# Layer two's weights through two buffers, products and last steps in another order, x loaded in pieces

## The chip, the cores and the metric

The kernel runs on one core of a Trainium2 chip. The core has a matrix engine (TensorE, PE in the rows; its weight loads are PEld), a vector engine (VectorE, DVE), a scalar engine (ScalarE, ACT), GpSimd (POOL) and SyncE (SP), which here issues nearly all DMAs. Each engine runs its own list of instructions in order, and semaphores tie the lists together. 16 DMA engines move the data between HBM and the core's on-chip memory. The metric is the device time of one execution in microseconds (us).

## What is computed

```python
x = attention(q, k, v)                # 4 batches, 8 heads, 576 rows, 64 columns; two kinds of window
x = x.transpose(0, 2, 1, 3).reshape(2304, 512)
h = x @ moe_w_in                      # 512 x 2048
x = (h - np.tanh(h)) @ moe_w_out      # 2048 x 512: layer one
h = x @ moe2_w_in                     # 512 x 2048
out = (h * (1 / (1 + np.exp(-h)))) @ moe2_w_out   # layer two
```

The weights come as 64-bit floats, which the kernel converts. Each operand of a product is held as two parts, a leading and a trailing one, and a product is three matmul passes (trailing with leading, leading with leading, leading with trailing): `passes`, L563.

## The kernel before

**Attention and layer one** come first. The 2304 tokens of layer one are cut into five blocks, four of 512 tokens and one of 256. For each block 16 slots run (f = 0 to 15), one for each 128 columns of w_in. In a slot PE makes h (12 matmuls, `hidden`), then the y products of the slot before (12 matmuls, `run_second`); ACT takes tanh (L589), DVE subtracts (L590), ACT copies the leading part of gg (L1213) and DVE subtracts the trailing part (L1215). At a block's end the four y banks in PSUM are cleared by ACT (L622) and DVE (L623) into x and stored to y1_hi and y1_lo.

**The feed stage.** Beside layer one's blocks 3 and 4 (340 to 455 us of the profile) layer two's w_in is prepared, and the results are stored to HBM as w2_in. `in_steps(i)` is called once in a slot, behind the slot's other work in the program. Each call converts one chunk of 128 columns (ACT L175 and L180, DVE L185, POOL L189, in the tile st_in). Two chunks make a pair q. On an even i the pair's three plain parts (ACT L1125 and L1126) and four sums and differences, the tile "mixed" (DVE L1128 and L1111), are made, the plain parts' trailing halves follow on DVE, the next two chunks are loaded, and plain is stored (L1137, L1138). On the odd i that follows the leading and trailing parts of mixed are made (ACT L1140, DVE L1111), and it is stored (L1142). So a pair is two slots and seven DMAs on SP's queue: four loads of 256 KB, two stores of 256 and 512 KB, one store of 1024 KB. There is one tile "mixed" and one tile "plain"; a pair can only write them when the last pair's stores have read them.

**Layer two** runs in three groups of 768 tokens, with the Winograd form of Strassen's scheme: seven products where eight would be needed. For each of eight quads (pairs of w_in chunks) `products` runs 7 products of 6 matmuls of 384 columns in the order 1, 6, 5, 7, 2, 3, 4 (`ORDER`); 1 and 2 add up in the bank a (h), 6 in b (q0), 5 and 3 in c (q1), 7 and 4 in d (y3). `sums` and `add` take values of the banks between the products (DVE L699): the sum with d has to read 7 alone, before 4 is added. In the first quad of the first group the last y products of layer one stand between the first three products and the others. Then 16 steps (f = 0 to 15, `second`) make the group's six output tiles, with 3 matmuls of 512 columns for each tile and step; `split` makes the leading and trailing parts gs of a later step (ACT L728, DVE L729), two steps ahead. In the last group steps 14 and 15 are run together, tile by tile. At the end each tile is copied (ot; ACT L756, DVE L754, or both for the last one) and stored.

**x of the next group.** While a group's 16 steps run, `load` fetches the next group's x (two halves XR[0] and XR[1], a leading and a trailing part of each, 768 KB a piece) and `mixes` returns 16 small steps (DVE L661, L665, L671; ACT L668) that make the operands "side" 5, 6 and 7, and the combined side 4 in place. The weights of each product or step are fetched to tiles wr by `fetch`, some steps ahead. In group 0 the w_out of layer two is also still being converted: each step there stores one converted chunk (room) and loads a raw one.

## Time and profile before

| | us |
|---|---|
| median of 3 runs | 873.75 |
| the runs | 871.97 to 874.69 |
| the profiled execution | 874.53 |
| its span, first to last instruction | 872.8 |
| PE busy in it | 849.9 |
| DVE, ACT, POOL busy | 521.0, 404.7, 125.3 |

The profile page gives busy times, the span in 40 slices, DMA queues, the chain of work that ended last, and groups of instructions by line. The trace behind it can be asked for one stretch, engine or line: what ran in order of time, and which wait preceded it. A row's duration on PE is modelled at its end; two rows in a sequence start closer together than the first one's duration says, so times on PE are best taken from start to start. "Idle before" in square brackets is how long the engine stood still before the row, and what ended that.

### The profile page before, as it was taken

The numbers are of one execution on the slowest core, as the hardware profiler recorded it, in microseconds if no ns is written. First come the engines' busy times: TensorE is split into PE (matmuls) and PEld (weight loads), VectorE is DVE, ScalarE is ACT, GpSimd is POOL, SyncE is SP. The second block draws the span as 40 slices with busy tenths as digits, with TensorE's granted clock in tenths as the row PEclk, the third lists the DMA queues.
The fourth block names the chain that finished last, engine by engine and source line by source line (L and its number), as shares of the span: only waits on it lengthen the run. The fifth ranks groups of instructions, "written<-read, shape, count | busy, mean of one in ns | idle before, by whom it ended". The sixth has DMA issues, their size and how long they took to land.

```text
span 872.8 us, 14406 instructions
## 1 busy us (share of the span) xinstructions
PE 849.9 (97%) x5287; PEld 730.0 (84%) x5287; DVE 521.0 (60%) x942; ACT 404.7 (46%) x939; POOL 125.3 (14%) x165
## 2 busy tenths in 40 slices
PE   8999999999999999998989999999999999999997
PEld 5777887888888888876779999887999888999885
DVE  3788996366677553655474677645666453566222
ACT  5899974344343433645443355663334231333112
POOL 8555441011000000111100011120000000000000
PEclk9999999999999999999999999999999999999999
DMA  9987263223342103675559199999796930998002
GB/s 233 273 225 182 68 152 122 67 49 56 63 129 50 36 21 97 229 255 184 224 225 379 62 371 375 335 385 366 265 407 229 359 111 2 350 359 266 1 0 73
DMA packets 148870, 166.63 MB, mean 191 GB/s; under 512 B 87840, under 2 KB 114496, under 8 KB 147776
## 3 DMA queue, kind: packets, MB, share of 16 engines
q1 hardware_dynamic: 147968, 164.86, 57.2%
q0 software_dynamic: 832, 0.85, 0.4%
q8 instruction: 42, 0.69, 0.3%
q14 instruction: 28, 0.23, 0.1%
HBM read 128.45 MB, written 37.22 MB: 190 GB/s over the span
## 4 chain that ended last, share of the span: by engine, by line
PE 76%; DMA 7%; ACT 7%; DVE 6%; issue 2%; SPq 2%; POOL 0%; DVEq 0%; ACTq 0%; POOLq 0%
PE y L563 34%; PE h L563 20%; PE q L563 15%; DMA w_in<-mixed 5%; DMA wr<-w_out 1%; ACT prob L454 1%; PE s L401 1%; PE h L495 1%; DVE g L590 1%; DVE x L623 1%; SPq L328 1%; ACT st L175 1%; DVE mixed L1111 1%; ACT mixed L1140 1%; PE o L401 1%
## 5 line engine op out<-in xcount | busy, mean ns | idle before, releaser
L563 PE MATMUL y<-gg,w 128*128 128x512 f32 (+1 forms) x960 | 220.8, 373 | 9.9 <-DVE gg L1215 9.9
L563 PE MATMUL h<-x,w 128*128 128x512 f32 (+1 forms) x960 | 218.8, 370 | 1.5 <-DVE g L590 0.9
L563 PEld LDWEIGHTS y<-gg,w 128*128 128x128 f32 x960 | 168.3, 190 | 44.6 <-DVE gg L1215 12.8
L563 PEld LDWEIGHTS h<-x,w 128*128 128x128 f32 x960 | 167.1, 189 | 33.3 <-POOL w L198 1.1
L563 PE MATMUL y<-wr,gs 128*128 128x512 f32 x576 | 139.6, 390 | 1.1 <-DMA wr<-w_out 0.6
L563 PEld LDWEIGHTS y<-wr,gs 128*128 128x128 f32 x576 | 107.9, 188 | 24.5 <-issue 1.0
L729 DVE TENSOR_TENSOR gs<-G,gs 128x768 fp32r<-128x768 f32 x48 | 45.7, 958 | 103.1 <-ACT gs L728 103.1
L728 ACT ACTIVATE gs<-G 128x768 fp32r<-128x768 f32 x48 | 40.3, 845 | 106.0 <-PE y L563 106.0
L708 ACT ACTIVATE G<-tmp 128x384 f32<-128x384 f32 x72 | 37.7, 526 | 102.1 <-DVE tmp L699 95.1
L563 PE MATMUL q<-x,wr 128*128 128x384 f32 x432 | 82.6, 334 | 0.0
L1213 ACT ACTIVATE gg<-g 128x512 fp32r<-128x512 f32 (+1 forms) x64 | 37.0, 578 | 94.9 <-DVE g L590 94.9
L563 PEld LDWEIGHTS q<-x,wr 128*128 128x128 f32 x432 | 75.6, 188 | 0.0
L563 PE MATMUL q<-wr,gs 128*128 128x512 f32 x288 | 72.9, 389 | 0.0
L589 ACT ACTIVATE g<-h 128x512 f32<-128x512 f32 (+1 forms) x64 | 34.7, 541 | 77.1 <-PE h L563 67.8
L590 DVE TENSOR_TENSOR g<-h,g 128x512 f32<-128x512 f32 (+1 forms) x64 | 39.7, 620 | 42.9 <-ACT g L589 42.4
L1215 DVE TENSOR_TENSOR gg<-g,gg 128x512 fp32r<-128x512 f32 (+1 forms) x64 | 40.1, 626 | 41.3 <-ACT gg L1213 39.9
L563 PEld LDWEIGHTS q<-wr,gs 128*128 128x128 f32 x288 | 54.1, 188 | 11.3
L563 PE MATMUL y<-x,wr 128*128 128x384 f32 x288 | 57.7, 334 | 0.9 <-DVE x L623 0.9
L563 PE MATMUL h<-x,wr 128*128 128x384 f32 x288 | 57.7, 334 | 0.0
L699 DVE TENSOR_TENSOR tmp<-tmp,q 128x384 f32<-128x384 f32 x72 | 39.7, 552 | 20.1 <-PE q L563 16.0
L563 PEld LDWEIGHTS y<-x,wr 128*128 128x128 f32 x288 | 50.6, 188 | 1.1 <-DVE x L623 1.1
L563 PEld LDWEIGHTS h<-x,wr 128*128 128x128 f32 x288 | 50.6, 188 | 0.2
(124 smaller groups left out, 975.4 us busy)
## 6 DMA issues: line engine op xcount, KB each, us to landing
wr<-w_in SPq DMA_DIRECT2D x72, 512.0 KB
wr<-w_out SPq DMA_DIRECT2D x48, 512.0 KB
st<-in_moe_w_in_dram SPq DMA_DIRECT2D x32, 256.0 KB
st<-in_moe_w_out_dram SPq DMA_DIRECT2D x16, 512.0 KB
st_in<-in_moe_w_in_dram SPq DMA_DIRECT2D x32, 256.0 KB
w_in<-mixed SPq DMA_DIRECT2D x8, 1024.0 KB
raw<-in_moe_w_out_dram SPq DMA_DIRECT2D x16, 512.0 KB
w_out<-room SPq DMA_DIRECT2D x16, 512.0 KB
```

Of the source, the lines that this page charges most:

```text
L175: engine.activation(out=high, in_=high, func=AF.Prelu, scale=2.0 ** -112, alpha=2.0 ** 32)
L328: out.append(lambda e, n=n, p0=p0, r=r, i=i, m=m: e.dma_start(out=self.vt[p0:p0 + m, :, n, :], in_=src[r, i:i + m]))
L401: nc.tensor.matmul(s[QB * j:QB * (j + 1), m, at:at + size], self.qT[64 * j:64 * j + 64, QB * n:QB * n + QB], self.kT[64 * j:64 * j + 64, k ...
L563: nc.tensor.matmul(o, stat[a], mov[b], start=first and n == 0, stop=last and n == 2, skip_group_check=more)
L589: nc.scalar.activation(out=g, in_=h, func=AF.Tanh)
L590: nc.vector.tensor_tensor(out=g, in0=h, in1=g, op=ALU.subtract)
L699: nc.vector.tensor_tensor(out=out, in0=a, in1=b, op=ALU.add)
L708: nc.scalar.activation(out=g, in_=h, func=AF.Tanh, scale=0.5)
L728: nc.scalar.activation(out=gs[:, 0], in_=g, func=AF.Copy)
L729: nc.vector.tensor_tensor(out=gs[:, 1], in0=g, in1=gs[:, 0].bitcast(F32), op=ALU.subtract)
L1213: nc.scalar.activation(out=gg[:, 0], in_=g, func=AF.Copy)
L1215: nc.vector.tensor_tensor(out=gg[:, 1], in0=g, in1=gg[:, 0].bitcast(F32), op=ALU.subtract)
```

## The change

1. mixed and plain get two tiles each, used by pairs in turn (q % 2).
2. In the first quad of the first group (`begins`) the products after layer one's last y run in the order 2, 3, 7, the sum with d, 4, instead of 7, the sum, 2, 3, 4.
3. `load` becomes `loads`, a list of four; XR[1] is loaded before XR[0], and the leading and the trailing part of one half follow each other. For group 0's own x all four are still issued together. For the next group's x one piece is issued in each of four steps, from step 5 on in group 0 (all four were issued at 7) and from step 0 on in group 1. Two mixing steps are run in each step from 8 on in group 0 (three each from 10 on before) and from 3 on in group 1 (two each from 2 on before).
4. Where two steps are run together (the last two of the last group), their parts are sorted: two tiles of step 14 run ahead of the first of step 15, and the tiles of the two steps alternate from there.
5. `dynamic_dma_scratch_size` is 2048 where it was 4096.

```diff
@@ -633,11 +633,12 @@
         def __init__(self, s):
             self.s, self.t0, self.G = s, 2 * HALF * s, []
 
-        def load(self):
-            for a, src in ((0, y1_hi), (1, y1_lo)):
-                for r, t in zip(XR, (self.t0, self.t0 + HALF)):
-                    nc.sync.dma_start(out=X[:, a, :, r].bitcast(F32),
-                                      in_=src[:, :, t:t + HALF].rearrange("c p t -> p c t"))
+        def loads(self):
+            def load(a, src, r, t):
+                return lambda: nc.sync.dma_start(out=X[:, a, :, r].bitcast(F32),
+                                                 in_=src[:, :, t:t + HALF].rearrange("c p t -> p c t"))
+
+            return [load(a, src, r, t) for r, t in zip(XR[::-1], (self.t0 + HALF, self.t0)) for a, src in ((0, y1_hi), (1, y1_lo))]
 
         def sides(self):
             a, b = (slice(0, 2), slice(2, 4))
@@ -736,11 +737,14 @@
                 self.y = [(ps_q.tile([P, 512], F32, tag=f"q{c - 3}", name=f"q{c - 3}") if c in (3, 4) else
                            ps_y.tile([P, 512], F32, tag=f"y{min(c, 3)}", name=f"y{min(c, 3)}")) for c in range(nt)]
             ws = [coming.pop(0) for _ in parts]
-            for c in range(nt):
+            order = [(c, k) for c in range(nt) for k in range(len(parts))]
+            if len(parts) > 1:
+                order.sort(key=lambda x: (x[0] + 2 * x[1], x[1]))
+            for c, k in order:
                 o = self.y[c]
-                for (f, gs), w in zip(parts, ws):
-                    passes(o, [gs[:, a, c * P:(c + 1) * P] for a in range(2)], [w[:, a] for a in range(2)],
-                           f == 0, f == NF - 1)
+                f, gs = parts[k]
+                passes(o, [gs[:, a, c * P:(c + 1) * P] for a in range(2)], [ws[k][:, a] for a in range(2)],
+                       f == 0, f == NF - 1)
                 if f == NF - 1:
                     ot = wpool.tile([P, DM], F32, tag="wout", name="ot")
                     t, p = self.t0 + c * P, 0
@@ -1119,6 +1123,7 @@
 
             q = i // 2 - 1
             own = 0 <= q < NF // 2
+            mixed, plain = mixes2[q % 2], plains[q % 2]
             if own and i % 2 == 0:
                 a, b = sides(q)
                 both = WIN[2 * q].high.bitcast(F32)
@@ -1173,8 +1178,8 @@
                 fpool = feeding.enter_context(tc.tile_pool(name="feed", bufs=1, reuse_waits="tile"))
                 ps_q = ctx.enter_context(tc.tile_pool(name="ps_q", bufs=1, space=PSUM, reuse_waits="tile"))
                 st_in = fpool.tile([P, 4, 2, DM // 2, 2], U32, name="st_in")
-                mixed = fpool.tile([P, 4, 2, 2 * P], F32R, name="mixed")
-                plain = fpool.tile([P, 3, 2, 2 * P], F32R, name="plain")
+                mixes2 = [fpool.tile([P, 4, 2, 2 * P], F32R, tag=f"mixed{k}", name="mixed") for k in range(2)]
+                plains = [fpool.tile([P, 3, 2, 2 * P], F32R, tag=f"plain{k}", name="plain") for k in range(2)]
                 for k in range(4):
                     WIN[k].load(st_in[:, k])
                 began = NF * (t - 1) + f + 1
@@ -1221,7 +1226,7 @@
                         in_steps(i - began)
                     if t == len(blocks) - 1:
                         if f == 4:
-                            groups[0].load()
+                            run(groups[0].loads())
                             mixing = groups[0].mixes()
                         if 5 < f < 14:
                             fetch()
@@ -1247,9 +1252,13 @@
                     begins = False
                     while waiting:
                         run_second()
-                u.products(quad, u.ORDER[3:4])
-                u.add(u.t[:, 1], u.t[:, 1], u.d)
-                u.products(quad, u.ORDER[4:])
+                    u.products(quad, (2, 3, 7))
+                    u.add(u.t[:, 1], u.t[:, 1], u.d)
+                    u.products(quad, (4,))
+                else:
+                    u.products(quad, u.ORDER[3:4])
+                    u.add(u.t[:, 1], u.t[:, 1], u.d)
+                    u.products(quad, u.ORDER[4:])
                 for _ in range(4 if u.s or quad < NF // 2 - 2 else 2):
                     fetch()
                 if quad == NF // 2 - 1:
@@ -1275,13 +1284,16 @@
                     out_split(k - 1)
                     out_steps(k)
                     out_load(k + 2)
-                if after and f == (0 if u.s else 7):
-                    after.load()
-                    mixing = after.mixes()
-                if f > (1 if u.s else 9):
-                    for _ in range(2 if u.s else 3):
-                        if mixing:
-                            mixing.pop(0)()
+                first = 0 if u.s else 5
+                if after and f == first:
+                    loading, mixing = after.loads(), after.mixes()
+                if after and f >= first:
+                    if loading:
+                        loading.pop(0)()
+                    if f > first + 2:
+                        for _ in range(2):
+                            if mixing:
+                                mixing.pop(0)()
             run(mixing)
 
 
@@ -1296,7 +1308,7 @@
     from concourse import mybir as _mybir
     from concourse.bass_utils import run_bass_kernel_spmd as _run
 
-    nc = _bacc.Bacc("TRN2", target_bir_lowering=False, num_devices=1, dynamic_dma_scratch_size=4096)
+    nc = _bacc.Bacc("TRN2", target_bir_lowering=False, num_devices=1, dynamic_dma_scratch_size=2048)
     arrays, args = {}, []
     for name in _INS:
         a = _np.ascontiguousarray(inputs[name])
```

Where instructions move, in the lists of the two programs:

DVE's list in the feed stage, the second pair (q = 1), before. L1128 is the first write to mixed, the L1111 with two halves (2x256) the first to plain; in square brackets are the queues that the instruction waits for (DMAHW: a DMA's).

```order
L1128 TENSOR_TENSOR mixed<-st_in 128x256 [waits DMAHW6_49,Pool_49]
L1111 TENSOR_TENSOR mixed<-st_in 128x256
L1111 TENSOR_TENSOR mixed<-mixed,st_in 128x256 [waits DVE_49]
L1111 TENSOR_TENSOR mixed<-st_in,mixed 128x256 [waits DVE_49]
L1111 TENSOR_TENSOR plain<-st_in,plain 128x2x256 [waits DMAHW5_49,DMAHW4_49,Activation_49]
L1111 TENSOR_TENSOR plain<-st_in,plain 128x256 [waits Activation_49]
L185 TENSOR_SCALAR st_in<-st_in 128x512 [waits DMAHW1_49,DMAHW0_49,Activation_49]
L590 TENSOR_TENSOR g<-h,g 128x512 [waits Activation_49]
L1215 TENSOR_TENSOR gg<-g,gg 128x512 [waits PE_49,Activation_49]
```

The same place now:

```order
L1133 TENSOR_TENSOR mixed<-st_in 128x256 [waits Pool_49]
L1115 TENSOR_TENSOR mixed<-st_in 128x256
L1115 TENSOR_TENSOR mixed<-mixed,st_in 128x256 [waits DVE_49]
L1115 TENSOR_TENSOR mixed<-st_in,mixed 128x256 [waits DVE_49]
L1115 TENSOR_TENSOR plain<-st_in,plain 128x2x256 [waits Activation_49]
L1115 TENSOR_TENSOR plain<-st_in,plain 128x256 [waits Activation_49]
L185 TENSOR_SCALAR st_in<-st_in 128x512 [waits DMAHW1_49,DMAHW0_49,Activation_49]
L590 TENSOR_TENSOR g<-h,g 128x512 [waits Activation_49]
L1220 TENSOR_TENSOR gg<-g,gg 128x512 [waits PE_49,Activation_49]
```

The order stays; the waits for the stores (DMAHW6; DMAHW5 and 4) are gone from this pair, and the third pair's L1133 waits for the store of the first.

DVE's list at the end of group 0, before: the last of the mixing steps (L661, L665, L671), the copies ot of three output tiles (L754), and the first sums of group 1 (L699). The L671 of 128x768 ahead of ot makes the trailing part of side 6, the one of 128x2x384 that of side 4.

```order
L671 TENSOR_TENSOR x_4370<-tmp,x_4370 128x768
L661 TENSOR_TENSOR tmp<-x 128x768
L665 TENSOR_TENSOR tmp<-tmp 128x768
L671 TENSOR_TENSOR x_4370<-tmp,x_4370 128x768
L754 TENSOR_SCALAR ot<-y_5503 128x512
L754 TENSOR_SCALAR ot<-q_5505 128x512
L754 TENSOR_SCALAR ot<-y_5507 128x512
L671 TENSOR_TENSOR x<-tmp,x 128x2x384
L699 TENSOR_TENSOR tmp<-tmp,q_6003 128x384
```

The same place now:

```order
L672 TENSOR_TENSOR x_4372<-tmp,x_4372 128x768
L662 TENSOR_TENSOR tmp<-x 128x768
L666 TENSOR_TENSOR tmp<-tmp 128x768
L758 TENSOR_SCALAR ot<-y_5505 128x512
L758 TENSOR_SCALAR ot<-q_5507 128x512
L758 TENSOR_SCALAR ot<-y_5509 128x512
L672 TENSOR_TENSOR x_4372<-tmp,x_4372 128x768
L672 TENSOR_TENSOR x<-tmp,x 128x2x384
L700 TENSOR_TENSOR tmp<-tmp,q_6005 128x384
```

Side 6's trailing part has moved behind the three copies.

PE's list in the last two steps of the last group, before (step 14's first tile, then step 15's first tile, then both steps' parts of each tile, six matmuls a row):

```order
L563 MATMUL y_7562<-wr,gs 128x512 [waits DMAHW5_49,Activation_49]
L563 MATMUL y_7562<-wr,gs 128x512
L563 MATMUL y_7562<-wr,gs 128x512 [waits DVE_49]
L563 MATMUL y_7562<-wr,gs 128x512 [waits DMAHW6_49,Activation_49]
L563 MATMUL y_7562<-wr,gs 128x512
L563 MATMUL y_7562<-wr,gs 128x512 [waits DVE_49]
L563 MATMUL y_7563<-wr,gs 128x512 x6
L563 MATMUL y_7564<-wr,gs 128x512 x6
L563 MATMUL q_7565<-wr,gs 128x512 x6
L563 MATMUL q_7566<-wr,gs 128x512 x6
L563 MATMUL y_7567<-wr,gs 128x512 x6
```

The same place now, from step 14's first tile on:

```order
L563 MATMUL y_7564<-wr,gs 128x512 [waits DVE_49]
L563 MATMUL y_7565<-wr,gs 128x512 x3
L563 MATMUL y_7566<-wr,gs 128x512 x3
L563 MATMUL y_7564<-wr,gs 128x512 [waits DMAHW6_49,Activation_49]
L563 MATMUL y_7564<-wr,gs 128x512
L563 MATMUL y_7564<-wr,gs 128x512 [waits DVE_49]
L563 MATMUL q_7567<-wr,gs 128x512 x3
L563 MATMUL y_7565<-wr,gs 128x512 x3
L563 MATMUL q_7568<-wr,gs 128x512 x3
L563 MATMUL y_7566<-wr,gs 128x512 x3
L563 MATMUL y_7569<-wr,gs 128x512 x3
```

Two tiles of step 14 now stand between its first tile and the waits for step 15's gs; the rest of the list (not shown) ends with step 15's parts of the last three tiles.

## Rows read from the trace of the kernel before

**Rows 1.** The page: busy us, share, instructions; PE's granted clock in 40 slices.
```profile
PE 849.9 (97%) x5287; PEld 730.0 (84%) x5287; DVE 521.0 (60%) x942; ACT 404.7 (46%) x939; POOL 125.3 (14%) x165
...
PEclk9999999999999999999999999999999999999999
```

**Rows 2.** Waits of PE (340-500 us) and DVE (340-460): us, times, longest.
```profile
PE y L563 <- DVE gg L1215: 9.1, 5, 1.9
...
DVE mixed L1128 <- DMA w_in<-mixed: 26.6, 7, 5.9
```

**Rows 3.** PE in order of time, feed stage: start, us, instruction, count, idle before.
```profile
379.69 2.88 PE L563 MATMUL y<-gg,w 128*128 128x512 f32 x12
382.41 2.88 PE L563 MATMUL h<-x,w 128*128 128x512 f32 x12
386.76 3.01 PE L563 MATMUL y<-gg,w 128*128 128x512 f32 x12 [1.46 <-DVE gg L1215]
389.61 2.88 PE L563 MATMUL h<-x,w 128*128 128x512 f32 x12
...
425.99 4.61 PE L563 MATMUL y<-gg,w 128*128 128x512 f32 x12 [1.89 <-DVE gg L1215]
430.43 2.90 PE L563 MATMUL h<-x,w 128*128 128x512 f32 x12
```

**Rows 4.** Busy by window: PE, PEld, DVE, ACT, POOL, granted clock, DMA share, GB/s.
```profile
427.00:428.00 1.00, 1.00 (x4) 0.81 (x3) 0.92 (x3) 0.79 (x2) 0.12 (x1) 0.50 0.80 232
```

**Rows 5.** The same view, two pairs of the feed stage, unstalled and stalled.
```profile
352.00:363.00 11.00, 11.00 (x50) 9.09 (x50) 7.74 (x15) 6.84 (x12) 2.28 (x3) 1.00 0.90 316
...
410.00:423.00 13.00, 11.11 (x49) 8.88 (x48) 6.95 (x14) 6.37 (x11) 2.08 (x2) 1.00 0.62 222
```

**Rows 6.** In order of time, from block 3 to block 4.
```profile
446.08 0.42 DVE L1128 TENSOR_TENSOR mixed<-st_in 128x256 f32<-128x256 f32 x1 [1.52 <-DMA w_in<-mixed]
...
450.62 2.41 PE L563 MATMUL y<-gg,w 128*128 128x256 f32 x12
...
453.90 1.69 PE L563 MATMUL h<-x,w 128*128 128x256 f32 x12 [0.86 <-DVE g L590]
...
455.42 1.60 PE L563 MATMUL y<-gg,w 128*128 128x256 f32 x12
```

**Rows 7.** In order of time, the first quad of group 0 (product 7 at 498.50).
```profile
498.50 1.31 PE L563 MATMUL y<-x,wr 128*128 128x384 f32 x6 [0.93 <-DVE x L623]
...
499.65 1.20 PE L563 MATMUL h<-x,wr 128*128 128x384 f32 x6
499.85 0.55 DVE L699 TENSOR_TENSOR tmp<-tmp,y 128x384 f32<-128x384 f32 x1 [1.40 <-PE y L563]
...
500.69 1.20 PE L563 MATMUL q<-x,wr 128*128 128x384 f32 x6
```

**Rows 8.** Group 0, step 12: a window's busy times; then in order of time.
```profile
560.00:580.00 20.00, 20.00 (x90) 16.57 (x89) 9.16 (x15) 12.38 (x21) 5.20 (x5) 1.00 1.01 386
...
592.50 1.73 SPq L1103 DMA_DIRECT2D wr<-w_out  x1
...
603.51 2.32 PE L563 MATMUL y<-wr,gs 128*128 128x512 f32 x9 [0.62 <-DMA wr<-w_out]
```

**Rows 9.** In order of time, from group 0 to group 1.
```profile
620.15 0.69 DVE L754 TENSOR_SCALAR ot<-y 128x512 f32<-128x512 f32 x1 [0.67 <-PE y L563]
620.76 0.95 DVE L671 TENSOR_TENSOR x<-tmp,x 128x768 fp32r<-128x768 f32 x1
...
621.02 2.24 PE L563 MATMUL q<-x,wr 128*128 128x384 f32 x12
```

**Rows 10.** PE in order of time, the last two steps.
```profile
858.29 1.52 PE L563 MATMUL y<-wr,gs 128*128 128x512 f32 x6
860.06 0.73 PE L563 MATMUL y<-wr,gs 128*128 128x512 f32 x2 [0.26 <-ACT gs L728]
861.05 3.24 PE L563 MATMUL y<-wr,gs 128*128 128x512 f32 x13 [0.26 <-DVE gs L729]
```

## The prediction, as it was put on record

> **What bounds the kernel now.** First the page: TensorE (PE) is busy 849.9 of 872.8 us, so at most some 23 us of idle can go, and its granted clock is full in nearly every slice [rows 1]. No edit here removes a matmul; the change can only win what PE waits for, and the slow matmuls that follow a wait. So the next view is PE's waits by stretch. From 340 to 500 us, the stage in which layer two's input weights are prepared beside layer one's blocks 3 and 4, PE waits 9.1 us for the vector engine's (DVE's) gg, in five stops, and the views of the other engines in that stage name what is behind: DVE stands 26.6 us at L1128, the first write to "mixed", until the DMA that stores the last pair's mixed has landed [rows 2]. Its queue runs in order. The gate of the next slot (L590, L1215) is queued behind L1128, and PE's y matmuls wait for the gate's gg. Then PE in order of time shows the size of a stop: 12 matmuls of 512 columns start 2.72 us after the 12 ahead of them (379.69 to 382.41), but the y at 386.76 starts 4.35 us after the h at 382.41, so 1.63 are lost [rows 3]. The last stage is read in the same way at its few stops.
>
> **Part 1, the two buffers (feed stage).** The five stops: 9.1 us of idle, plus 0.16 each, since the view counts a row of 12 as 2.88 long and the next starts after 2.72: 9.1 + 0.8 = 9.9. After a stop the first 12 take 0.13 longer (386.76 to 389.61 is 2.85 against 2.72), four times: 0.5. After the fourth stop the 12 at 425.99 take 4.44 us (to 430.43), 1.72 too many [rows 3]; the granted clock there reads 0.50, that is 1.2 of 2.4 GHz, after the 1.89 us in which PE stood idle [rows 4]. Together 9.9 + 0.5 + 1.7 = 12.1 us.
>
> Is something else late next? With two buffers the mixed of pair q waits for the store of pair q-2, a whole pair (10.9 us) longer, where the longest single wait was 5.9 us [rows 2]. The stretch 352 to 363 is a whole pair run before any store is waited for: PE busy 11.00 of 11.00, DVE 7.74, ACT 6.84, and the 16 DMA engines 0.90 with two stores of layer one's y in it; the stalled pair from 410 to 423 has the same instructions, PE 11.11 of 13.00 and DMA share 0.62 [rows 5]. 0.62 x 13 = 8.1 us of DMA work fit into 10.9 us (74%). SyncE's (SP's) queue then issues the same seven DMAs a pair, earlier. I take all 12.1; the ends are 5.6 (half of it is spent on a new wait, the rival below) and 12.1.
>
> At the step from block 3 to block 4, 12 matmuls of 256 columns take 1.5 us (453.90 to 455.42), but the y at 450.62 lasts 2.41 (0.9 lost, waiting bank by bank for DVE's L623), and the next h waits 0.86 more for L590 [rows 6]. All of it is DVE and ACT running late, and 1.52 us of that lateness is one more wait at L1128. But the slots are half as long there and DVE holds more work than they last, so the whole 1.8 won't go. Between 0 and 1.8 I take 1.0, nearer to the 1.5 that DVE gets back.
>
> **Part 2, the first pair's products.** In the first quad product 7 needs the bank y3, which DVE's L623 clears late: PE waits 0.93 at 498.50. With 2 and 3 (6 matmuls each, 1.04 us by the starts at 499.65 and 500.69) ahead of 7 that wait is covered. But the sum that DVE makes of 7's bank then stands directly ahead of 4, which writes the same bank: DVE begins 0.20 after 7 has left PE (499.65 to 499.85) and takes 0.55 [rows 7], and PE starts about 0.05 later, 0.8 us in all. 0.93 and 0.11 for the slow first matmuls, less 0.8: 0.2 us won, with -0.3 (a late DVE) and 1.0 (no wait at all) as ends.
>
> **Part 3, x loads in pieces.** In group 0 PE waits 0.62 at 603.51 (0.78 by starts) for a tile of w_out whose load was issued at 592.50, behind all four x loads (3 MB, issued together); the DMA engines are full there, 1.01 from 560 on [rows 8]. After the change only three of the four pieces are ahead of that tile. One piece is 0.79 MB, at 386 GB/s 2.0 us, more than the 0.8 by which it came late: 0.8 won, ends 0 and 0.9. The Trainium skill, "Perfetto Trace Analysis", DMA Optimizations, says that splitting DMAs may let some start sooner if the DMA engines are generally idle; they aren't here, so by that rule nothing is won and the sum would be 0.8 us higher. The row decides for me, since the bytes stay the same and only their order changes.
>
> The same edit spreads the 16 mixing steps of the next x over slots 8 to 15, two each, where they stood three each from slot 10. The last two now fall in slot 15, behind the three output copies on DVE. Before, x2's side 6 was long done there. Now DVE's last copy (620.15, about 0.6 to the next start) comes first and side 6's trailing part (0.95, as the step at 620.76 is) runs from about 620.8 to 621.7; PE wants it in the first matmul of product 6, at 621.02 [rows 9]. That is a new wait of 0.7 us, ends 0.5 and 0.9. Between groups 1 and 2 the mixing ends at slot 10 of 16: nothing.
>
> **Part 4, the last two steps.** PE has done step 14's first tile when it needs step 15's gs, for which ACT and DVE are still working: 2 matmuls run at 860.06 and the rest go on at 861.05, while they would have begun at 859.65 (858.29 and six matmuls of 0.227) [rows 10]. 0.41 + (0.99 - 0.45) = 0.95 us lost. In the new order two more tiles of step 14 (1.36 us) lie ahead, so PE gets there at 861.0: about 0.9 is won. Behind it the last tile's two copies follow one after the other as before. Three tiles now finish in the last 1.4 us where they had 2.7, so the last store may queue behind two others; I take 0.85, ends 0 and 0.95.
>
> **The sum**, against the profiled execution: 874.53 us (span 872.8, 1.7 around it), which is 0.8 above the median of 873.75. 12.1 + 1.0 + 0.2 + 0.8 - 0.7 + 0.85 = 14.25, so 874.5 - 14.3 = **860.2 us**. With every term at its bad end but the first at 12.1: 12.1 + 0 - 0.3 + 0 - 0.9 + 0 = 10.9, 863.6; with every good end 12.1 + 1.8 + 1.0 + 0.9 - 0.5 + 0.95 = 16.25, 858.3.
>
> **Rivals.**
> 1. *A new wait takes half the feed stage's gain.* Stores and loads overlap once the waits are gone, a load of st_in or DVE's turn comes late, and a pair settles near 12 us instead of 10.9: 6 x 1.1 = 6.5 us back, 866.7. For it: 2.88 MB a pair in 10.9 us is 265 GB/s, where the stalled pair moved 222. Against it: the pair from 352 to 363 [rows 5], which moved 316 GB/s with no stop.
> 2. *The pieces starve group 0 of weights (slower than before).* SP's queue runs in order, and each piece stands ahead of the next weight tile in a stage that has no DMA time left [rows 8]. If every slot from 6 to 15 came to wait for one piece's 2.0 us, 20.5 us would be added: 860.2 + 0.8 + 20.5 = 881.5. From 1.4 us a slot on it ends slower than before ((874.5 - 861.0) / 10). Against it: there are four pieces and not ten, and the tiles are asked for four slots (16 us) ahead.
> 3. *The change doesn't do what it says*: the second buffer is waited for like the first, and only parts 2 to 4 count: 0.2 + 0.8 - 0.7 + 0.85 = 1.15, 873.4. Against it: in the new program the second pair's L1128 no longer names a DMA among its waits.
> 4. *The order of the last two steps costs the clock.* PE changes its bank every 3 matmuls there, as it did before in all other steps of this stage, at full clock; were it to run those 12 groups at 1.2 GHz, 12 x 0.68 = 8.2 us would come on top: 868.4. By the Trainium skill, "TensorE: Matmul & The Clock Gate", A second HAM failure mode, cycling through PSUM banks makes the clock go up and down; the trace does not bear it out here, since the clock reads 9 (full) in the slices of all steps that cycle so [rows 1].
>
> **How the numbers follow.** Forecast 860.2: 0.82. Rival 1: 0.13, rival 2: 0.02, rival 3: 0.02, rival 4: 0.01. The range for 8 in 10 takes in the forecast's ends and part of rival 1, and 0.8 below for the median under the profiled time: 857.0 to 865.0. About 0.3% (2.6 us) is what a measurement can tell from no change; faster by more than that are the forecast and rivals 1 and 4: 0.96; within it rival 3: 0.02; slower rival 2: 0.02.
>
> **What would show it.** Right: between 352 and 440 us PE has no wait for gg, and DVE none at "mixed" for a DMA; the granted clock has no slice under full there; block 4 begins some 12 us earlier; PE waits about 0.7 us for DVE at product 6 of group 1's first quad and about 0.8 at product 4 of group 0's; no wait for w_out's tiles; PE's last two steps without a stop. Wrong: pairs longer than 11 us in the feed stage with a DMA or st_in as releaser, PE waiting for wr in group 0's second half, or a lower clock.

## The result and the profile after

The changed kernel takes **858.62 us** (median of 4 runs, 858.05 to 860.15) where the kernel before takes 872.91 on the same chip (4 runs, 871.97 to 874.69). The ratio is 0.9837, with a 95% interval of 0.9814 to 0.9859: 14.3 us faster. Its profiled execution took 858.44 us with a span of 856.6, which is 16.1 shorter than the profiled span before.

The page of the changed kernel: busy us, share of the span and instructions of each engine, and PE's granted clock in 40 slices; then the shares of the chain that ended last, which on the page of before held PE 76% and the DMA w_in<-mixed 5%.

```profile
PE 843.8 (99%) x5287; PEld 728.7 (85%) x5287; DVE 520.0 (61%) x942; ACT 404.9 (47%) x939; POOL 125.2 (15%) x165
...
PEclk9999999999999999999999999999999999999999
...
PE 92%; DMA 4%; DVE 1%; ACT 1%; issue 0%; SPq 0%; POOL 0%; DVEq 0%; POOLq 0%
```

It answers to [rows 1]: the same 5287 matmuls, 6.1 us less of PE's busy time (a PE that runs slowly after a stop counts as busy) and about 10 us less idle.

**The feed stage.** DVE's waits of the changed kernel from 335 to 445 us (us in total, times, longest); PE has none at all in that stretch. Then PE in order of time, then busy time by window (PE, PEld, DVE, ACT, POOL, granted clock, DMA share, GB/s).

```profile
DVE g L590 <- ACT g L589: 26.2, 20, 3.4
DVE gg L1220 <- ACT gg L1218: 13.6, 21, 0.7
DVE mixed L1115 <- ACT mixed L1145: 1.8, 7, 0.3
DVE gg L1220 <- PE y L563: 1.4, 2, 0.7
```

```profile
381.17 2.88 PE L563 MATMUL h<-x,w 128*128 128x512 f32 x12
383.89 2.88 PE L563 MATMUL y<-gg,w 128*128 128x512 f32 x12
386.61 2.88 PE L563 MATMUL h<-x,w 128*128 128x512 f32 x12
```

```profile
380.00:400.00 20.00, 20.00 (x90) 16.54 (x89) 12.97 (x24) 12.49 (x21) 3.12 (x3) 1.00 0.77 278
427.00:428.00 1.00, 1.00 (x6) 0.84 (x5) 0.00 (x0) 0.39 (x1) 0.87 (x1) 1.00 0.94 393
```

The 26.6 us that DVE stood at "mixed" for the DMA [rows 2] are gone, and what DVE now waits for is the normal turn of a slot: PE's h, ACT's tanh, its own gate. Every 12 matmuls of PE start 2.72 us after the 12 ahead of them, where [rows 3] had stops of up to 1.89. The clock at 427 reads 1.00 and not 0.50 [rows 4].

**Block 3 to block 4**, in order of time, PE and DVE's first write to mixed there:

```profile
430.13 1.60 PE L563 MATMUL h<-x,w 128*128 128x256 f32 x12
430.24 0.42 DVE L1133 TENSOR_TENSOR mixed<-st_in 128x256 f32<-128x256 f32 x1
...
434.31 3.04 PE L563 MATMUL h<-x,w 128*128 128x256 f32 x24
437.18 1.60 PE L563 MATMUL y<-gg,w 128*128 128x256 f32 x12
```

No row of PE has an idle time in brackets any more, and the y lasts 1.60 where it lasted 2.41 [rows 6].

**The first quad of group 0, then the first quad of group 1**, in order of time:

```profile
482.05 1.21 PE L563 MATMUL h<-x,wr 128*128 128x384 f32 x6
...
484.14 1.21 PE L563 MATMUL y<-x,wr 128*128 128x384 f32 x6
...
485.38 0.56 DVE L700 TENSOR_TENSOR tmp<-tmp,y 128x384 f32<-128x384 f32 x1 [2.29 <-PE y L563]
...
485.99 1.31 PE L563 MATMUL y<-x,wr 128*128 128x384 f32 x6 [0.65 <-DVE tmp L700]
```

```profile
603.43 1.22 PE L563 MATMUL h<-x,wr 128*128 128x384 f32 x6
603.63 0.69 DVE L758 TENSOR_SCALAR ot<-y 128x512 f32<-128x512 f32 x1 [0.67 <-PE y L563]
604.24 1.82 DVE L672 TENSOR_TENSOR x<-tmp,x 128x768 fp32r<-128x768 f32 x2
605.24 2.35 PE L563 MATMUL q<-x,wr 128*128 128x384 f32 x12 [0.59 <-DVE x L672]
```

Both forecast waits are there. Product 7 (484.14) no longer waits [rows 7], but product 4 (485.99) stands 0.65 for the sum with d. And product 6 of group 1 (605.24) stands 0.59 for side 6's trailing part, the first of the two L672, which DVE makes behind the last output copy [rows 9].

**The end**, in order of time:

```profile
842.62 3.56 PE L563 MATMUL y<-wr,gs 128*128 128x512 f32 x15
...
850.78 0.84 PE L563 MATMUL y<-wr,gs 128*128 128x512 f32 x3
...
852.08 0.42 DVE L756 TENSOR_SCALAR ot<-y 128x256 f32<-128x256 f32 x1 [1.08 <-ACT ot L755]
```

PE's last two steps run without the two stops of [rows 10]. But from the end of the last copy (852.50) to the end of the span now pass 4.1 us; before, DVE's last copy of this kind began at 868.83 and ended at 869.25, 3.5 ahead of the end.

To account for all of it, I take the start of the same matmul, by its place in PE's list, in both traces, and so cut the span into stretches. Stretches that agree in all runs to 0.02 us are left out of the table: block 4, group 0 from its second quad to its step 11, and groups 1 and 2 (234.00 us).

| stretch, us | before | after | change |
|---|---|---|---|
| start of the run to block 3's feed stage | 357.70 | 356.46 | -1.24 |
| feed stage | 85.62 | 73.44 | -12.18 |
| block 3 to block 4 | 11.85 | 9.92 | -1.93 |
| first quad of group 0 | 11.42 | 11.15 | -0.27 |
| group 0, step 11 to the end (w_out) | 21.98 | 21.08 | -0.90 |
| start of group 1 (side 6) | 3.20 | 4.06 | +0.86 |
| last two steps | 11.06 | 9.97 | -1.09 |
| last matmul's start to the span's end | 4.78 | 5.40 | +0.62 |
| sum | | | -16.13 |

### The profile page after: what moved, and what is told of

Same layout as the page of the kernel before. It is cut to its first block, busy times and chain, and to the rows that moved or that the text cites. A ratio compares the mean times of both kernels' runs of the same rounds, so it can differ in the third digit from the quotient of the medians.

```text
span 856.6 us, 14406 instructions
## 1 busy us (share of the span) xinstructions
PE 843.8 (99%) x5287; PEld 728.7 (85%) x5287; DVE 520.0 (61%) x942; ACT 404.9 (47%) x939; POOL 125.2 (15%) x165
## 4 chain that ended last, share of the span: by engine, by line
PE 92%; DMA 4%; DVE 1%; ACT 1%; issue 0%; SPq 0%; POOL 0%; DVEq 0%; POOLq 0%
PE y L563 44%; PE h L563 28%; PE q L563 16%; DMA st<-in_moe_w_in_dram 2%; PE s L401 1%; DMA kin<-in_k_dram 1%; PE h L495 1%; PE o L401 1%; DMA qin<-in_q_dram 1%; PE s L495 0%; ACT prob L454 0%; PE o L495 0%; DVE x L623 0%; ACT x L622 0%; DVE g L590 0%
## 5 line engine op out<-in xcount | busy, mean ns | idle before, releaser
L563 PE MATMUL y<-gg,w 128*128 128x512 f32 (+1 forms) x960 | 217.7, 369 | 0.8 <-DVE gg L1220 0.7
```

Of the source, the lines that this page charges most:

```text
L563: nc.tensor.matmul(o, stat[a], mov[b], start=first and n == 0, stop=last and n == 2, skip_group_check=more)
```

## The experiments

Each run was taken beside the kernel before on its chip, which took 871.9 to 872.1 us there. "Total" is one time, or the median where an interval stands with it; the other columns are the stretches of the table above. A run's total follows the start of the run too, which no edit here touches and which varies by some us (last section), so verdicts on terms under 1 us come from the stretches.

| run | total | start | feed | 3 to 4 | quad | w_out | side 6 | last steps | tail |
|---|---|---|---|---|---|---|---|---|---|
| e1 | 860.28 | 357.94 | 73.44 | 9.92 | 11.43 | 21.59 | 3.20 | 11.07 | 4.77 |
| e2 | 871.97 | 356.04 | 85.08 | 11.87 | 11.16 | 21.41 | 4.06 | 9.97 | 5.42 |
| e3 | 859.71 | 357.68 | 73.44 | 9.92 | 11.16 | 21.08 | 4.05 | 9.97 | 5.44 |
| e4 | 871.96 | 356.52 | 85.85 | 10.51 | 11.17 | 21.65 | 4.05 | 9.97 | 5.32 |
| e5 | 859.53 | 357.19 | 73.44 | 9.92 | 11.16 | 21.08 | 4.05 | 9.97 | 5.79 |
| e6 | 861.88 | 360.73 | 73.44 | 9.92 | 11.15 | 21.08 | 3.20 | 9.97 | 5.42 |
| e7 | 859.62 | 358.41 | 73.44 | 9.92 | 10.41 | 21.08 | 4.05 | 9.97 | 5.41 |
| e8 | 858.98 | 357.61 | 73.44 | 9.92 | 11.16 | 21.08 | 4.05 | 9.97 | 4.79 |
| e9 | 857.0 | 356.87 | 73.44 | 9.92 | 10.41 | 21.13 | 3.20 | 9.97 | 4.93 |
| e10 | 858.5 | 355.78 | 73.44 | 9.92 | 11.15 | 21.08 | 4.07 | 9.97 | 5.52 |
| e11 | 860.13 | 357.08 | 73.44 | 9.92 | 11.15 | 22.91 | 3.20 | 9.97 | 5.41 |
| e12 | 859.51 | 357.07 | 73.44 | 9.92 | 11.15 | 22.51 | 3.20 | 9.97 | 5.27 |

### e1 and e2: the buffers apart from all else

e1 is the kernel before with the two buffers and the smaller scratch; e2 is the changed kernel with one tile each.

```diff
 # e1, from the kernel before (and dynamic_dma_scratch_size=2048)
+            mixed, plain = mixes2[q % 2], plains[q % 2]
-                mixed = fpool.tile(...)
-                plain = fpool.tile(...)
+                mixes2 = [fpool.tile(..., tag=f"mixed{k}", name="mixed") for k in range(2)]
+                plains = [fpool.tile(..., tag=f"plain{k}", name="plain") for k in range(2)]
 # e2, from the changed kernel: the same lines the other way, scratch left at 2048
```

> The kernel before with only the two tiles each for mixed and plain (and the smaller scratch that makes room for them). Theory: the buffers alone carry the gain, 12.2 us in the feed stage and 1.9 at the step from block 3 to block 4, so 14 us under the kernel before, about 858.8 us; PE has no wait for gg in the feed stage, but still 0.9 us at product 7 of the first quad, 0.6 for a w_out tile in group 0 and two stops in the last two steps. Rival: part of the gain at the step to block 4 came from the x loads' other order, then the 1.9 us stay and it is 860.7 us.

> The changed kernel with one tile each for mixed and plain again; the other three parts stay. Theory: those three parts sum to 0.3 + 0.9 - 0.85 + 0.5 = 0.85 us under the kernel before, about 872 us; five stops of PE for gg are back. Rival: the other parts help or hurt the feed stage too, then it lies 2 us or more from that.

The feed stage and the step to block 4 of e1 are those of the changed kernel to the hundredth (73.44, 9.92), so the buffers bring 14.1 us by themselves against the profile of before. By the totals, one time each, e1 lies only 11.6 us under the kernel before (860.28 and 871.87). Its start of the run is 1.48 longer than that of the changed kernel, and the run of before beside it has no trace, so the total settles the size less well than the stretches do. All other edits together bring what is left: from e1 to the changed kernel the stretches behind block 4 change by -0.28 (quad), -0.51 (w_out), +0.86, -1.10 and +0.63, which is -0.40. e2 has the smaller scratch and loses the gain (85.08, 11.87, against 85.62 and 11.85), so the scratch does not explain it. Waits of e2's DVE from 335 to 445 us:

```profile
DVE mixed L1132 <- DMA w_in<-mixed: 26.1, 7, 4.8
```

That is the wait of [rows 2] with its seven stops, back with the single tile.

### e3 and e4: which of the two second tiles

```diff
 # e3: two tiles mixed, one plain (the list plains is made one tile long as well)
-            mixed, plain = mixes2[q % 2], plains[q % 2]
+            mixed, plain = mixes2[q % 2], plains[0]
 # e4: one tile mixed, two plain (the list mixes2 is made one tile long as well)
+            mixed, plain = mixes2[0], plains[q % 2]
```

> The changed kernel with two tiles for mixed and one for plain. Theory: only mixed's tile was in the way; plain's stores are issued some 3 us after its first write and landed within 6 more, so they are done before the next pair (10.9 us) writes: no new wait of PE, 858.6 us as the changed kernel. Rival: plain's wait takes the place of mixed's (ACT stood 13 us for it in the kernel before), then ACT waits for w_in<-plain, PE stops again and it is 861 us or more.

> The changed kernel with one tile for mixed and two for plain. Theory: DVE waits some 26 us for mixed's stores as in the kernel before and PE makes five stops: 872 us. Rival: each of the two tiles carries part of the gain: 863 to 868 us.

The second mixed tile does it alone. Waits in the same stretch, e3's ACT first, then e4's DVE and PE:

```profile
ACT plain L1130 <- DMA w_in<-plain: 2.6, 3, 1.0
```

```profile
DVE mixed L1133 <- DMA w_in<-mixed: 25.4, 7, 4.8
PE y L563 <- DVE gg L1220: 9.5, 5, 2.4
```

With a single plain tile ACT does wait for plain's store, 2.6 us in three stops, and PE's feed stage is 73.44 all the same: ACT has that much room in a slot. With a single mixed tile the feed stage is about as long as before (85.62), with two plain tiles (85.85 in e4) or one (85.08 in e2).

The step to block 4 takes 10.51 in e4 and 11.87 in e2, but that is no gain of the second plain tile. ACT writes plain in that step without a wait in e2 too. What differs is PE's last y row of the feed stage: in e4 it ran at half clock, so PE came to the step later, and the same lateness of DVE cost it less there. e2's last y row and its ACT in the step, then e4's y row and its busy time by window:

```profile
438.48 3.04 PE L563 MATMUL y<-gg,w 128*128 128x512 f32 x12 [1.84 <-DVE gg L1219]
...
441.55 0.66 ACT L1129 ACTIVATE plain<-st_in 128x512 fp32r<-128x512 f32 x1
```

```profile
438.36 4.39 PE L563 MATMUL y<-gg,w 128*128 128x512 f32 x12 [2.37 <-DVE gg L1220]
```

```profile
439.00:440.00 1.00, 1.00 (x4) 0.81 (x3) 1.00 (x2) 1.00 (x3) 0.00 (x0) 0.50 0.00 0
```

Both stretches together take 97.47 us before, 96.95 in e2 and 96.36 in e4, against 83.36 with two mixed tiles. So by these traces the second mixed tile is worth 13.0 to 14.1 us, and no run shows a worth of the second plain tile.

### e5: does a pair just fit?

The prediction's first rival was that the freed pair settles on the DMA engines. e5 gives them 1 MB more a pair: mixed is stored a second time, to a place of its own, behind the first store. Nothing is left out.

```diff
                 nc.sync.dma_start(out=w2_in[q, :, 1:5], in_=mixed...)
+                nc.sync.dma_start(out=spare[q], in_=mixed...)
```

> The changed kernel with each pair's mixed stored a second time, to a spare place in HBM: 1 MB more a pair, 3.9 MB in all. Theory: in the changed kernel the DMA engines have room in the feed stage (share 0.77 of the window from 380 to 400 us, 8.4 us of a pair's 10.9); 1 MB more at the 420 GB/s of a burst is 2.5 us, which just fills the pair: PE makes no stop or a few small ones, at most 3 us in all, 858 to 862 us. Rival: the stage was near a DMA limit already, then each of the pairs is longer than 11.5 us and it is over 863 us.

Busy time by window, e5 (the window of the changed kernel shown above has a DMA share of 0.77 and 278 GB/s):

```profile
380.00:400.00 20.00, 20.00 (x90) 16.56 (x89) 12.94 (x24) 12.48 (x21) 3.68 (x4) 1.00 1.00 369
```

The DMA engines are full, and PE is busy 20.00 of 20.00 us; the feed stage takes 73.44. So the pair does not stand at an edge: a third more traffic costs nothing, and the rival falls.

### e6, e7, e8: the three places that gave something back

e6 runs three mixing steps in steps 12 and 13 of the groups, so that the last is done by step 14. e7 puts 7 between 2 and 3, so that product 3 lies between 7 and the product that waits for 7's sum. e8 keeps three tiles of step 14 ahead of step 15 (three, as the list of PE shows, and not the two that "The change" speaks of) but runs the last three tiles one after the other, so that their copies and stores are 1.36 us apart and not together.

```diff
 # e6
-                        for _ in range(2):
+                        for _ in range(3 if f in (12, 13) else 2):
                             if mixing:
 # e7
-                    u.products(quad, (2, 3, 7))
+                    u.products(quad, (2, 7, 3))
 # e8
-                order.sort(key=lambda x: (x[0] + 2 * x[1], x[1]))
+                order = [(c, k) for cs in ((0, 1, 2), (3,), (4,), (5,)) for k in range(2) for c in cs]
```

> The changed kernel with three mixing steps each in steps 12 and 13 of a group, so that the mixing ends in step 14, ahead of the output copies. Theory: the 0.6 us that PE waits for side 6 (L672) at the start of group 1 go; from the first h of group 1's first quad to its q it is 1.07 us in place of 1.81, and 0.85 us in all: 857.6 us. Rival: the denser steps make gs late and PE waits for gs at steps 14 or 15 of group 0, then nothing is won.

> The changed kernel with product 7 between 2 and 3 in the first quad. Theory: the bank y3 is clear when 2 has run (L623 ended at 483.10, 2 at 483.10), and 3 covers the sum that 4 waits for: from the first matmul of 2 to the next quad's first h it is 4.2 us in place of 5.10, 857.8 us. Rival: 7 comes too early and PE waits for L623 in place of the sum, then less than 0.3 us is won.

> The changed kernel with another order of the last two steps: step 14's parts of tiles 0, 1, 2, then step 15's parts of them, then both parts of 3, of 4, of 5. Theory: step 15's gs is still covered, PE ends as early as in the changed kernel, and the tiles end 1.36 us apart, so that the last store isn't queued: from the end of PE to the end of the span 0.5 us less, 858.0 us. Rival: the tail is the store's own time, and nothing changes.

The places in order of time, e6 (products 1 and 6 of group 1), then e7 (products 2, 7, 3 and 4 of group 0):

```profile
607.72 1.23 PE L563 MATMUL h<-x,wr 128*128 128x384 f32 x6
...
608.79 2.24 PE L563 MATMUL q<-x,wr 128*128 128x384 f32 x12
```

```profile
484.00 1.21 PE L563 MATMUL h<-x,wr 128*128 128x384 f32 x6
...
485.09 1.33 PE L563 MATMUL y<-x,wr 128*128 128x384 f32 x6
...
486.26 1.21 PE L563 MATMUL q<-x,wr 128*128 128x384 f32 x6
...
487.31 1.20 PE L563 MATMUL y<-x,wr 128*128 128x384 f32 x6
```

In e6 product 6 starts 1.07 us behind product 1 where it started 1.81 behind it, and the stretch is back at 3.20, the value of before. In e7 product 4 follows product 3 after 1.05 us without a wait, and the quad takes 10.41, 0.74 less. Both are what the stretch of the changed kernel had lost. In e8 the tail is 4.79, that of before (4.78), with PE's last two steps as short as in the changed kernel (9.97). The last copies of e8, in order of time:

```profile
852.80 0.38 ACT L755 ACTIVATE ot<-y 128x256 f32<-128x256 f32 x1 [0.76 <-PE y L563]
853.22 0.42 DVE L756 TENSOR_SCALAR ot<-y 128x256 f32<-128x256 f32 x1 [2.44 <-ACT ot L755]
```

They end at 853.64, and the span of 857.2 ends 3.5 us later, as before. In all 14 profiles the tail goes with the order of the last two steps: 5.27 to 5.79 in the ten that have the changed order, 4.77 to 4.93 in the kernel before, e1, e8 and e9. e6's total of 861.88 is no verdict on the edit: its start of the run took 360.73, 4.27 more than in the changed kernel's profile, and 861.88 less 4.27 is 857.6, the time that was expected.

### e9 and e10: the three together, beside the changed kernel again

e9 is the changed kernel with all three edits; e10 is the changed kernel itself, both in five rounds on one chip.

> The changed kernel with the three edits of the last runs together: mixing done by step 14, products in the order 2, 7, 3, the last tiles spaced. Theory: they stand in different stages and add up, 0.86 + 0.75 + 0.48 = 2.1 us under the changed kernel in the stretches concerned, 856.5 us median. Rival: the earlier stages' gain is lost again at a later wait, then it is within 1 us of the changed kernel.

> The changed kernel again, beside the one with three more edits, on the same chip: 858.6 us median, and 14.3 us under the kernel before. The part of the run up to the feed stage (attention and layer one's first blocks) differs from run to run by some us whatever the kernel; the stretches behind it do not.

e9 took 857.0 us (4 runs, 856.06 to 858.09), 0.9823 of the kernel before with an interval of 0.9803 to 0.9843. e10 took 858.5 (5 runs, 857.89 to 861.58), 0.9848 with 0.9825 to 0.9871 (13.5 us under the 872.03 beside it), so the first result repeats. In the stretches e9 has all three gains beside each other: 0.74 and 0.87 and 0.59. The medians differ by 1.5 us in the same direction; the two intervals overlap, so by the times alone e9 is only probably the faster one. PE has six waits in e9 over the whole span. The two largest:

```profile
PE y L886 <- DVE warm L882: 1.5, 1, 1.5
PE y L486 <- POOL prob L464: 1.1, 1, 1.1
...
```

All six lie ahead of 335 us, so in the stages that this change touches PE has no wait left.

### e11 and e12: the x loads together again

The changed kernel with the old timing of the loads (all four at step 7) and of the mixing; the order of the four within `loads` stays the new one. e12 repeats e11.

```diff
-                first = 0 if u.s else 5
-                if after and f == first:
-                    loading, mixing = after.loads(), after.mixes()
-                ...
+                if after and f == (0 if u.s else 7):
+                    run(after.loads())
+                    mixing = after.mixes()
+                if f > (1 if u.s else 9):
+                    for _ in range(2 if u.s else 3):
+                        ...
```

> The changed kernel with the x loads of the next group issued together again (step 7 of group 0, step 0 of group 1, XR[1] first) and the mixing at its old steps. Theory: the part on the x loads wins about 0.5 to 0.9 us in group 0 (no wait for a w_out tile) and loses 0.86 at the start of group 1, so together it is worth nothing: from group 0's step 11 to group 1's first h 21.6 to 22.0 us in place of 21.08, and from there to the third product 3.20 in place of 4.06. Rival: without the pieces the stage stalls more than in the kernel before, since it runs into it sooner: over 22.3 us.

> The kernel with the x loads issued together a second time: its wait for a w_out tile in group 0 was 1.6 us, where the kernel with the buffers alone had 0.2 and the kernel before 0.6. If the wait's size belongs to the kernel, it is again 22.9 us from group 0's step 11 to group 1's first h; if it changes from run to run, it is some other value between 21.2 and 23.

e11's issue of the tile that is waited for and PE in order of time, then the same row of PE in e12, then the two rows in e1:

```profile
577.26 2.48 SPq L1107 DMA_DIRECT2D wr<-w_out  x1
...
589.43 2.32 PE L563 MATMUL y<-wr,gs 128*128 128x512 f32 x9 [1.55 <-DMA wr<-w_out]
```

```profile
589.08 2.29 PE L563 MATMUL y<-wr,gs 128*128 128x512 f32 x9 [1.18 <-DMA wr<-w_out]
```

```profile
578.58 1.67 SPq L1103 DMA_DIRECT2D wr<-w_out  x1
...
589.27 2.31 PE L563 MATMUL y<-wr,gs 128*128 128x512 f32 x9 [0.25 <-DMA wr<-w_out]
```

And the changed kernel's issues of the same tile and of the fourth piece of x:

```profile
574.33 0.51 SPq L1107 DMA_DIRECT2D wr<-w_out  x1
...
578.19 0.37 SPq L638 DMA_DIRECT2D x<-y_lo  x1
```

The wait for w_out [rows 8] is back as soon as the four loads stand together, and the wait for side 6 is gone (3.20). So the pieces win 1.83 and 1.43 us against e11 and e12 in the w_out stretch, and 0.5 to 0.9 against e1 and the kernel before, which load in the old order. e11 and e12 are one kernel and differ by 0.40, so the 0.39 between e1 and the kernel before may be spread alone. What is left open is why e11 and e12 wait more than e1 does. The place of the tile in the queue does not differ: in e1 the tile is issued at 578.58, 9.6 us ahead of the three matmuls that PE still has (588.18), in e11 at 577.26, 9.8 ahead of them (587.04). But from its issue to PE's next matmul pass 12.2 us in e11 (577.26 to 589.43) and 10.7 in e1 (578.58 to 589.27). 0.8 of that is SP's issue itself, which lasts 2.48 and 1.67. It is the same transfer behind the same 3 MB, whose halves come in another order. The difference came twice, and no run here changes that order alone.

The pieces have a second cost, which shows in e2 and e4 only. There too PE has no wait for w_out, but the stretch takes 21.41 and 21.65 in place of 21.08. The last piece is issued later than the four loads were, the mixing step that reads it waits on DVE, and gs is queued behind that step. In order of time, the changed kernel's step, then e4's step, its gs and PE:

```profile
588.15 0.96 DVE L662 TENSOR_TENSOR tmp<-x 128x768 f32<-128x768 f32 x1 [2.86 <-DMA x<-y_lo]
```

```profile
602.23 0.96 DVE L662 TENSOR_TENSOR tmp<-x 128x768 f32<-128x768 f32 x1 [2.78 <-DMA x<-y_lo]
...
604.09 0.95 DVE L730 TENSOR_TENSOR gs<-G,gs 128x768 fp32r<-128x768 f32 x1
...
605.10 1.90 PE L563 MATMUL y<-wr,gs 128*128 128x512 f32 x7 [0.23 <-DVE gs L730]
```

In the changed kernel the same wait stands on DVE, and gs still comes in time.

## Why the prediction was right

Forecast 860.2, measured 858.62. The medians differ by 14.3 us, the forecast's own number, but that is partly luck: the sum below comes to 14.89, the profiled pair differs by 16.1, and e10 came out at 13.5. By the steps of the sum:

| term | forecast | measured | shown by |
|---|---|---|---|
| feed stage | 12.1 | 12.18 | e1, e2 |
| block 3 to block 4 | 1.0 | 1.93 | e1 |
| first quad | 0.2 | 0.27 | the traces, e7 |
| w_out | 0.8 | 0.90 | e11, e12 |
| side 6 | -0.7 | -0.86 | e6 |
| last two steps | 0.85 | 0.47 | e8 |
| sum | 14.25 | 14.89 | |

**The feed stage** carried the prediction, and its step held: count what each stop costs from start to start, the slow matmuls behind it and the one stretch at half clock, and look whether an unstalled pair with the same work fits. The traces confirm the releaser (DVE's wait is gone and PE's with it), e1 and e2 that the buffers are the cause, e5 that the next limit is farther away than the unstalled pair showed. One term of it is less fixed than the forecast made it. A row at half clock stood behind a different stop in each of the three traces with a single mixed tile: behind the fourth before (12 matmuls in 4.44 us after 1.89 of idle), the first in e2 (4.29 after 2.29) and the fifth in e4 (4.23 after 2.37). Stops of 1.91 before (2.85 for the next 12) and 2.07 in e4 (2.88) had none. The prediction gave the credit to two new tiles; e3 shows that the second plain tile is idle weight.

**The step to block 4** was the term that was mis-sized. The prediction named 1.8 us of loss there and took 1.0, because slots half as long seemed to keep DVE late by themselves. They do not: with two mixed tiles DVE is in time there, in e3 with a single plain tile as well (9.92), so all of it was lateness carried over from the wait at mixed, and 1.93 came back. The row that decided was in reach: 1.52 us of wait at mixed stood in [rows 6] just ahead of the stop. How the loss falls to the feed stage and to this step depends on when PE gets there (10.51 in e4, behind the half-clock row), so the two terms are best read together: forecast 13.1, measured 14.11.

**The end** was mis-sized the other way. PE won 1.09 (forecast 0.9), but the tail grew by 0.62, of which the prediction had taken off 0.05. It had named the reason, three tiles that finish in the last 1.4 us, and priced it far too low. e8 shows that it is the order alone: with the same start of step 15 and the tiles spaced, the tail is 4.79.

**The new waits** came where the order of instructions said: 0.65 us at product 4 and 0.59 at product 6 in brackets, and 0.86 by starts for the second one (forecast 0.7, ends 0.5 and 0.9), for the slow first matmuls behind a wait are not in the brackets.

**The pieces.** The Trainium skill, "Perfetto Trace Analysis", DMA Optimizations, says that splitting transfers may let some start sooner and, where the DMA engines are generally idle, the whole task end sooner. Of splitting where the engines are full it says nothing, so "by that rule nothing is won" went beyond what it states. Here they were at 1.01 [rows 8], the four loads stayed as large as they were and were only spread over four steps, and the stretch won 0.90 all the same, 1.43 and 1.83 against e12 and e11: the urgent tile went to the queue at 574.33, ahead of the fourth piece (578.19) as forecast, 12.8 us before PE used it (587.11) in place of 11.0 before. Rival 2's "16 us ahead" is not what [rows 8] show (592.50 to 603.51); in the changed kernel PE waited for no tile all the same. Two products in the rivals are a little off: 6 x 1.1 is 6.6 and not 6.5 (rival 1), and ten pieces of 2.0 us are 20 and not 20.5 (rival 2).

**The clock.** Beside rival 4 the prediction names the Trainium skill, "TensorE: Matmul & The Clock Gate", A second HAM failure mode. The Trainium skill tells there of one bf16 kernel that cycles through PSUM banks, where PE idles briefly between groups of matmuls and the clock goes up and down. The last two steps of the changed kernel change the bank every 3 matmuls, and the granted clock reads 1.00 from 840 to 852 us, the higher of its two levels (2.4 GHz), so the trace does not show the effect here.

The rest of the difference is not a term of the sum. The profiled execution that it was made against (874.53) lay 1.6 us above the median of before (872.91), and the start of the run accounts for 1.24 of the 16.13.

## What to carry to other kernels

When an engine's first write to a tile waits for the store that reads it, the wait is handed on: everything queued behind it on that engine comes late, and with it the engine that bounds the kernel (26.6 us of DVE's waits cost PE some 14 here); a second tile for the one late write was enough, so test each tile alone before paying memory for all. Price such a stop from start to start and include the lateness that it hands on to a later, denser stretch, which came back whole here. The order that ended several tiles together shortened the compute and lengthened the stores behind it, so keep the last results spaced.

## What the runs showed of the hardware

- The time of a run is set early. Up to block 3's feed stage, in code that no edit touches, the 14 profiles took 355.78 to 360.73 us, while the 234.00 us of groups 1 and 2 were the same in all of them. The slowest start has a wait of PE that the profile puts down to nothing it shows (2.4 us in e6, 1.8 in e7, 1.3 in e1, none in the changed kernel's profile), which is part of the spread only. e6, waits of PE from 0 to 120 us:

```profile
PE s L495 <- issue: 2.4, 1, 2.4
```

  Changes of under 2 us are better read from stretches cut at the same matmul than from totals.
- A DMA share of 1.00 at 369 GB/s for 20 us cost PE nothing in e5, while a share of 1.01 at 375 GB/s (e11, 560 to 590 us) made PE wait. The share says that the engines are full, not that anyone waits for what they carry; that has to be read from the waits.
